# Paired query-key products, one pool of PSUM banks in two-bank tiles, and a new order of work in an adaLN attention and token-MLP block

## Chip, cores and metric

One core of one Trainium2 chip runs the whole block. The time is the device time of one execution in microseconds; a program's time is the median of its runs. Where a sentence below or in the prediction speaks of a span, it is the profiled execution's, from the first to the last thing in the trace.

## What is computed

The input x has 2048 rows of 512. With B = 1, 32 heads of 16, a window of 8 keys at distances 0, 2, ..., 14:

```
sa, ca, ga, sb, cb, gb = silu(c) @ w_mod
h = layernorm(x) * (1 + ca) + sa
q, k, v = h @ wqkv                              # 32 heads of 16
logits[s, w] = q[s] . k[s - 2 w] / 4            # w = 0..7, rows before the first masked
x = x + ga * ((softmax(logits) . v[s - 2 w]) @ wo)
h = layernorm(layernorm(x) * (1 + cb) + sb)
u = gelu(h^T @ w1 + b1)                         # over rows: 2048 -> 1792
x = x + gb * (u @ w2 + b2)^T                    # 1792 -> 2048
```

## The kernel before

Rows are held in 16 tiles of 128 (tile 0 is rows 0 to 127). Attention goes by five chunks of 2, 4, 4, 4 and 2 tiles (`SIZES`), numbered 0 to 4. In each chunk:

- PE (TensorE) makes q, k and v in 512-column products (lines 701 to 742); ACT (ScalarE) and a few times DVE (VectorE) bring them from PSUM to SBUF ("ev" in the names).
- DVE multiplies q with the eight shifted k, once for each of four groups of head dimensions (`qk3_2` is group 2 of chunk 3, line 758 on): 128x4096 elements an instruction in chunks of 4 tiles, 128x2048 in those of 2. PE sums the groups (`red`, 775) into the logits, two banks `psL` that no other work uses.
- DVE takes the maximum (`max`, 794), PE subtracts it (`sub`), ACT takes the exponential (`exp`), PE and ACT make the reciprocal (`esum`, `rcp`), DVE scales (`smB`).
- Four small copies (`a2`, 826) spread the weights, and DVE multiplies them with v (`pv`), PE sums over the window (`pvacc`), ACT brings the result to SBUF (`oev`).
- PE makes the output projection of a tile (`wo`), ACT or DVE adds the gated residual (`x1`); with the residual left out of the projection (suffix n), DVE adds it.
- Then come the second norm: statistics (`ln2q`), root (`rstd2`), bias (`nb2`), the norm (`n2`), the scale and shift of DVE (`aff`, 903, one entry of two instructions); and the third norm (`ln3s`, `rstd3`, `nb3`, `h3`).

MLP1 (922 to 984) sums over rows. Its 14 column tiles f of 128 go in two sweeps of seven, each over parts of the rows; a sum that is interrupted is parked: ACT or DVE copies it from PSUM to SBUF (`park`), and it is put back by PE (`inj`) or added by DVE (`padd`). ACT applies gelu at the end. MLP2 (986 to 1042) makes 16 output tiles, DVE finishes each (`fin`, two instructions), and SP (SyncE) issues the store (`st_out`).

Two tables set the order. `ORDER` (192 to 250) is a list of tokens, written out, of all operations: `:a`, `:d`, `:p`, `:s` name the engine, `:q` has PE do a product as four of 32 columns side by side (lines 541 to 545), n leaves the residual out, `fill:n` is n dummy products. The program is emitted in that order, engine by engine. `schedule()` (86 to 126) gives each operation that needs a PSUM bank the slot that was freed longest ago (line 116). The pool of slots has six banks, each a tile of its own (`psS0` to `psS5`, line 313):

```
psS = [psp.tile([P, 512], F32, name=f"psS{i}") for i in range(6)]
psL = psp.tile([P, 2, 512], F32, name="psL")
```

The framework then makes the semaphore waits between engines from the tiles that instructions read and write.

Of the kernel before, what the change touches and what calls it, by code (L numbers as in the profile page):

```python
# [211 lines left out]
pvacc1_2 qkv3_10:q halo_v3:a oev1_2:a ev3_10:a qkv3_02:q qkv3_20:q pv1_1 qkv3_01:q pvacc1_1 esum2:q ev3_02:a ev3_20:a
ev3_22:a aff0 pv1_0 qkv3_03:q qkv3_00:q pvacc1_0 pv1_3 oev1_1:a ev3_01:a rcp2 halo_k3:a smB2 ln3s0 qkv3_11:q oev1_0:a
pvacc1_3 ev3_11:a oev1_3:a qkv3_23:q fill:1:q wo5:q wo3:q qk3_2 qk3_1 ld_w1_0_0 ld_w1_0_512 vd2_3 xt14 vd2_2 vd2_1
a2_2_1:s a2_2_0:s a2_2_2:s vd2_0 a2_2_3:s wo4:q ln3s1 ev3_03:a ev3_00:a qk3_0 x1_3:a x1_4:a qk3_3 ln2q3 ln2q4 x1_5:a
ev3_23:a qkv4_22:q qkv3_21:q ev3_21:a wo2:q red3_0 x1_2:a qkv4_20:q fill:2:q red3_1 qkv4_00:q red3_2 ev4_22:a ln2q5
ln2q2 ev4_20:a rstd2_2 pv2_0 rstd2_4 red3_3 pvacc2_0 oev2_0:a pv2_3 qkv4_12:q ev4_12:a qkv4_02:q nb2_2 ev4_02:a n2_2:a
max3 sub3:q pvacc2_3 exp3 esum3:q oev2_3:a rstd3_0 pv2_2 nb2_4 pvacc2_2 qkv4_10:q rcp3 n2_5:a oev2_2:a n2_4:a pv2_1
pvacc2_1 fill:4:q oev2_1:a wo6:q wo7:q wo8:q wo9:q ev4_00:a smB3 n2_3:p vd3_3 ld_w1_0_896 vd3_1 vd3_0 a2_3_2:s a2_3_3:s
a2_3_0:s a2_3_1:s vd3_2 ld_w2_1 aff2 nb3_0 aff4 h3_1:p h3_0:p halo_v4:p ln3s3:a ln3s2:d ln3s4:d ln3v3 ln3v2 ln3v4  # L220
ln3s5:a ln3v5 pv3_1 x1_8:a x1_7:a x1_6:a rstd3_2 ev4_10:a h3_3 h3_2 mlp1_0_1_0 mlp1_0_2_0 mlp1_0_5_0:q mlp1_0_3_0:q
pvacc3_1 rstd3_4 nb3_4 x1_9:a pv3_2 pv3_3 pv3_0 h3_4:a h3_5:a oev3_1:a mlp1_0_2_2:q mlp1_0_1_2:q mlp1_0_0_0:q
mlp1_0_0_2:q mlp1_0_3_2:q mlp1_0_0_4:q mlp1_0_5_2:q mlp1_0_5_4:q mlp1_0_3_4:q mlp1_0_1_4:q pvacc3_2 mlp1_0_2_4:q ln2q9
ln2q6 park0_0:a park0_1:a ln2q7 park0_2:a oev3_2:a qk4_0 qk4_2 mlp1_0_4_0:q mlp1_0_4_2:q pvacc3_3 mlp1_0_6_0:q ln2q8
oev3_3:a mlp1_0_6_2:q pvacc3_0 mlp1_0_6_4:q mlp1_0_4_4:q oev3_0:a mlp1_0_7_0:q wo13:qn red4_0 rstd2_6 nb2_6 park0_3:a
qk4_1 x1_13:d n2_9:a n2_6:a park0_4:a wo12:q n2_8:p ld_w1_0_1152 ld_w1_0_1408 vd4_1 ld_w2_3 vd4_2 vd4_0 vd4_3 n2_7:d
qk4_3 wo11:q red4_1 red4_2 red4_3 ln2q13 x1_12:a ln2q12 park0_5:a x1_11:a rstd2_12 aff6 ln3s7:a mlp1_0_9_0 mlp1_0_9_2
mlp1_0_8_0 mlp1_0_9_4 wo10:n max4 nb2_12 sub4 exp4 park0_6:a ln3s9:d ln3s8:d ln3v8 ln3v9 esum4 ln3s6:d ln3v7 rcp4 ln3v6
smB4 rstd3_6 mlp1_0_7_2 mlp1_0_8_2 mlp1_0_10_0 mlp1_0_10_2 mlp1_0_12_0 mlp1_0_12_2 mlp1_0_8_4 mlp1_0_10_4 mlp1_0_7_4
mlp1_0_12_4 a2_4_1:s a2_4_2:s a2_4_3:s n2_13:p x1_10:d nb3_6 h3_8:d h3_6:d h3_7:d a2_4_0:a h3_9:a ln2q10 ln2q11  # L230
rstd2_10 n2_12:d aff12 mlp1_0_11_0 mlp1_0_11_2 mlp1_0_11_4 mlp1_0_8_6 mlp1_0_7_6 pv4_1 nb2_10 pv4_2 pv4_0 ln3s13
# [10 lines left out]
padd2_1 gelu1 gelu4 mlp1_2_3_11 mlp1_2_3_14 mlp1_2_2_14 mlp1_2_6_11 padd2_3 padd2_2 gelu2 padd2_6 gelu6 gelu3
mlp1_1_12_10 mlp1_2_5_11 mlp1_2_5_14 mlp1_1_11_10 padd2_5 padd1_11 gelu5 gelu9 padd1_12 mlp1_1_13_10 gelu12 gelu11
mlp2_0_0 padd1_13 gelu13 ld_w2_4 ld_w2_2 ld_w2_5 mlp2_0_0b ld_w2_7 ld_w2_9 ld_w2_11 ld_w2_13 mlp2_2_0 mlp2_6_0
mlp2_0_0c mlp2_3_0 mlp2_8_0 mlp2_4_0 fin0_0 st_out0_0 fin4_0 fin2_0 st_out2_0 fin6_0 st_out4_0 fpre gsc mlp2_9_0 fin3_0
fin8_0 st_out8_0 st_out6_0 mlp2_5_0 mlp2_1_0 fin1_0 mlp2_14_0 mlp2_10_0 st_out1_0 st_out3_0 fin5_0 ld_w2_15 fin10_0
# [7 lines left out]
def kernel(  # L254
# [379 lines left out]
    def build_chunk(ch):  # L634
# [126 lines left out]
        for dlo in range(4):  # L761
            s_ = _Slot("big")

            def prod(s_=s_):
                return big_r[s_.i][:, 0:NW * C].rearrange("p (q w s) -> p q w s", q=4, w=NW)

            def f(dlo=dlo, prod=prod):
                qv = _ap(q_sb[:, dlo, 0:1], [[0, NW], [SB, 4], [1, SB]])
                kv = _ap(k_c[:, dlo, PAD:PAD + 1], [[-DIL, NW], [SB, 4], [1, SB]])
                nc.vector.tensor_tensor(_ap(prod()[:, 0, 0, 0:1], [[SB, NW], [NW * SB, 4], [1, SB]]), qv, kv,  # L770
                                        op=ALU.mult)
            add("dve", _t_tt2(NW * C), f, reads=[("q", bq, dlo), ("k", ch, dlo), ("kq", ch)] + ([("kh", 3)] if ch == 3 else [("k", ch - 1, dlo)]), alloc=s_,
                locks=True, name=f"qk{ch}_{dlo}")

            def f(dlo=dlo, prod=prod):
                for hf in range(NW // WPM):
                    for jj in range(4):
                        nc.tensor.matmul(psL[32 * jj:32 * jj + 32, hf, 0:WPM * SB], lhsT=group4[:],
                                         rhs=prod()[:, jj, hf * WPM:(hf + 1) * WPM, :], start=(dlo == 0),
                                         stop=(dlo == 3), tile_position=(0, 32 * jj))  # L780
# [297 lines left out]
```

## Time and profile before

| what | value |
|---|---|
| median of 3 runs | 198.61 us (198.4 to 198.69) |
| profiled execution | 198.75 us, span 197.0 us, granted clock 0.997 |
| PE busy | 185.8 us of the span |
| DVE busy | 157.3 us |
| ACT busy | 127.1 us |
| POOL (GpSimd) busy | 22.8 us |
| moved by DMA | 36.02 MB |

All instructions are issued by one helper, so lines of the profile carry the line number 143; groups are told apart by their tiles: big holds DVE's products, psS the PSUM banks, gT the parked sums, h, hT and the like the norms. PE is the matmul engine and PEld its weight loads, which overlap it. A column "idle before" with "<-" names what ended the wait of an engine.

### The profile page before, as it was taken

To read this page: it belongs to the slowest core of one execution; us is meant where nothing else is said; L and a number is where in the kernel's file an instruction comes from. 1 tells how busy PE (TensorE), PEld (TensorE's weight loads), DVE (VectorE), ACT (ScalarE), POOL (GpSimd) and SP (SyncE) were. 2 spreads that over 40 slices of the span, in tenths; PEclk is the share of its full clock that TensorE was granted. 3 is DMA by queue.
4 is the path that set the end of the run, shared out by engine and by line. 5 is a ranking of instruction groups with operands and counts; after the bars stand their busy time and mean duration, and the time that the engine had idled before them with its cause. 6 is when DMAs were issued, how large, how long until landed. Compare 5 with 4: busy or idle time off the path is not lost.

```text
span 197.0 us, 5568 instructions
## 1 busy us (share of the span) xinstructions
PE 185.8 (94%) x2331; PEld 99.5 (50%) x2343; DVE 157.3 (80%) x222; ACT 127.1 (64%) x304; POOL 22.8 (12%) x46
## 2 busy tenths in 40 slices
PE   3999999999999996899999999999999999999993
PEld 1476656565465674435554454444444444444462
DVE  2789999999999999999999999977550207864693
ACT  4799999898999999999997899735660000000000
POOL 4184003000500001130031000500000000000000
PEclk9999999999999999999999999999999999999998
DMA  5999695888997449180497494588999200144113
GB/s 156 357 355 341 226 259 137 101 201 253 302 303 268 149 144 322 34 218 14 136 245 208 91 255 97 157 273 177 290 348 339 61 0 15 38 130 99 53 53 107
DMA packets 53893, 36.02 MB, mean 183 GB/s; under 512 B 24428, under 2 KB 50668, under 8 KB 53868
## 3 DMA queue, kind: packets, MB, share of 16 engines
q1 hardware_dynamic: 52772, 35.27, 64.2%
q10 hardware_dynamic: 1096, 0.39, 0.8%
q8 instruction: 18, 0.29, 0.6%
q14 instruction: 7, 0.06, 0.1%
HBM read 22.55 MB, written 2.10 MB: 125 GB/s over the span
## 4 chain that ended last, share of the span: by engine, by line
PE 63%; DVE 21%; issue 5%; DMA 4%; SPq 3%; ACT 2%; DVEq 0%; ACTq 0%
PE psS L143 61%; DVE big L143 14%; DMA xx<-in_A_x_dram 4%; DVE h L143 4%; SPq L143 3%; PE psL L143 2%; DVE lsb L143 1%; DVE st L143 1%; ACT xx L143 1%; ACT junk L143 1%; DVE m L143 1%; DVE nb L143 0%; ACT k_f L143 0%; DVE woq L143 0%; ACT rs L143 0%
## 5 line engine op out<-in xcount | busy, mean ns | idle before, releaser
L143 PEld LDWEIGHTS <-wst 128*128 128x128 bf16 (+1 forms) x578 | 35.6, 101 | 32.7 <-issue 2.8
L143 PE MATMUL psS<-h,wst 128*32 128x512 bf16 (+1 forms) x350 | 50.1, 379 | 0.4 <-issue 0.2
L143 DVE TENSOR_TENSOR big<-a2sb,vD 128x4096 bf16<-128x4096 bf16 (+1 forms) x20 | 36.4, 1857 | 0.1
L143 DVE TENSOR_TENSOR big<-q_sb,k_f 128x4096 bf16<-128x4096 bf16 (+1 forms) x20 | 36.3, 1857 | 0.0
L143 PE MATMUL psS<-hT,w_qkv 128*32 128x512 bf16 (+1 forms) x576 | 29.0, 344 | 0.0
L143 DVE SCALAR_TENSOR_TENSOR h<-psS,bcol,rows_bc 128x512 f32<-128x512 f32 (+2 forms) x17 | 12.1, 709 | 21.2 <-PE psS L143 21.0
L143 PEld LDWEIGHTS <-w_qkv 128*32 128x32 bf16 (+1 forms) x618 | 21.2, 107 | 13.9
L143 PE MATMUL psS<-gT,big 128*128 128x512 bf16 x111 | 24.8, 379 | 0.1
L143 POOL TENSOR_SCALAR h<-xx,rs,nb 128x512 bf16<-128x512 bf16 x11 | 11.5, 1047 | 94.3 <-DVE nb L143 40.6
L143 PEld LDWEIGHTS <-big 128*128 128x128 bf16 x144 | 12.1, 98 | 13.8 <-DMA big<-in_w_mod_dram 0.5
L143 PE MATMUL psS<-woq,o_sb 128*32 128x512 bf16 (+1 forms) x220 | 16.7, 379 | 0.3 <-ACT o_sb L143 0.3
L143 ACT ACTIVATE gT<-psS,bcol 128x512 bf16<-128x512 f32 x14 | 8.9, 685 | 8.6 <-DVE psS L143 8.6
L143 DVE TENSOR_TENSOR psS<-psS,gT 128x512 f32<-128x512 f32 x14 | 9.4, 697 | 5.5 <-PE psS L143 5.5
L143 DVE TENSOR_TENSOR h<-h,xx 128x512 bf16<-128x512 f32 (+2 forms) x17 | 11.1, 652 | 2.6 <-DMA out_dram<-h 2.1
L143 PE MATMUL psS<-hT,wst 128*32 128x512 bf16 (+2 forms) x134 | 11.8, 355 | 0.2
L143 DVE TENSOR_TENSOR h<-h,rows_bc 128x1024 bf16<-128x1024 bf16 (+2 forms) x16 | 11.5, 718 | 0.5
L143 ACT ACTIVATE v_sb<-psS,qvb 128x512 bf16<-128x512 f32 (+1 forms) x20 | 11.1, 599 | 0.7 <-PE psS L143 0.7
L143 DVE BATCH_NORM_STATS2 st<-xx 128x6 f32<-128x512 bf16 x12 | 7.9, 681 | 4.5 <-DMA xx<-in_A_x_dram 4.5
L143 PEld LDWEIGHTS <-group 128*32 128x32 bf16 x288 | 7.7, 96 | 7.3 <-DVE big L143 1.7
L143 PE MATMUL psS<-big,group 128*32 128x512 bf16 (+1 forms) x160 | 9.9, 338 | 1.1 <-DVE big L143 0.8
L143 ACT ACTIVATE q_sb<-psS,qvb 128x512 bf16<-128x512 f32 (+1 forms) x18 | 10.6, 614 | 0.4 <-PE psS L143 0.3
L143 PEld LDWEIGHTS <-o_sb 128*32 128x32 bf16 (+1 forms) x220 | 7.0, 97 | 7.1 <-ACT o_sb L143 0.8
(106 smaller groups left out, 249.3 us busy)
## 6 DMA issues: line engine op xcount, KB each, us to landing
vD<-v_sb SPq DMA_DIRECT2D x12, 524.5 KB, 5.1
big<-in_B_w_dram SPq DMA_DIRECT2D x4, 896.0 KB, 8.3
vD<-v_sb SPq DMA_DIRECT2D x8, 268.5 KB, 2.5
wst<-in_B_w_dram SPq DMA_DIRECT2D x3, 640.0 KB, 4.4
out_dram<-h SPq DMA_DIRECT2D x15, 128.0 KB, 1.8
wst<-in_B_w_dram SPq DMA_DIRECT2D x2, 800.0 KB, 5.4
xx<-in_A_x_dram SPq DMA_DIRECT2D x6, 256.0 KB, 7.2
gT<-in_w_mod_dram SPq DMA_DIRECT2D x4, 384.0 KB, 7.6
```

The source lines that it names most:

```text
L143: r = fn(*a, **k)
```

## The change

Four things change.

1. *Pairs.* In chunks 3 and 4 one DVE instruction makes the products of two groups (128x8192 and 128x4096 elements); the product lies in the order window, row in all chunks, so the reduction reads it in runs of 128. The ring of four product buffers becomes two tiles of two.
2. *Scale and shift singly.* `aff` becomes `afm` and `afs`, so that other DVE work can stand between them.
3. *One pool of PSUM banks.* The pool has eight slots in four tiles of two banks, psT0 to psT3: slot i is half i mod 2 of tile i div 2. Logits take one slot in chunks 0 and 4, and an aligned pair in the others, instead of `psL`.
4. *Order.* Tokens up to the first output projection (`wo1`) are as before; behind it the list is new. `wo11` and `wo12` leave the residual to DVE, two more of chunk 3's copies and one other of chunk 4's go out from ACT, more products are done four-way.

```
-    G = _Graph(dict(ps=6, big=NBIG, vd=NVD))
+    G = _Graph(dict(ps=8, big=NBIG, vd=NVD))
...
-    psS = [psp.tile([P, 512], F32, name=f"psS{i}") for i in range(6)]
-    psL = psp.tile([P, 2, 512], F32, name="psL")
+    psT = [psp.tile([P, 2, 512], F32, name=f"psT{i}") for i in range(4)]
 
     def ps(slot):
-        return psS[slot.i][:]
+        return psT[slot.i // 2][:, slot.i % 2, :]
...
-    big_r = ring(NBIG, [P, NW * CM], BF, "big")
+    big_t = ring(NBIG // 2, [P, 2, NW * CM], BF, "big")
+    big_r = [big_t[i // 2][:, i % 2, :] for i in range(NBIG)]
...
+        NQ = 2 if ch in QKP else 1
+        for d0 in range(0, 4, NQ):
+            s_ = _Slot("big", NQ * C // CM or 1)
...
+            def f(d0=d0, prod=prod):
+                qv = _ap(q_sb[:, d0, 0:1], [[C, NQ], [0, NW], [1, C]])
+                k0, k1 = k_c[:, 0, PAD:PAD + 1], k_c[:, 1, PAD:PAD + 1]
+                kv = _ap(k_c[:, d0, PAD:PAD + 1], [[k1.offset - k0.offset, NQ], [-DIL, NW], [1, C]])
+                nc.vector.tensor_tensor(prod(), qv, kv, op=ALU.mult)
...
-                nc.vector.tensor_tensor(hv, hv, ab_bc[:].unsqueeze(1).to_broadcast([P, gn, D]), op=ALU.mult)
-                nc.vector.tensor_tensor(hv, hv, sb_bc[:].unsqueeze(1).to_broadcast([P, gn, D]), op=ALU.add)
...
+            for nm, row, rk, op_ in (("afm", ab_bc, "ab_bc", ALU.mult), ("afs", sb_bc, "sb_bc", ALU.add)):
...
-x1_1:a wo0:q x1_0:a ln2q1 xt10 xt12 red2_0 qkv2_23:q qkv3_22:q qkv3_12:q vd1_0 st_row1 vd1_2 ev2_23:a ln2q0 rstd2_0
...
+st_row1 vd1_1 vd1_2 xt10 ld_row1 a2_1_3:s a2_1_0:s xt12 a2_1_2:s vd1_3 vd1_0 red2_0 wo1:q x1_1:a wo0:q ln2q1 qkv2_21:q
...
```

The rows below are the program's, in each engine's order; the numbers behind names tell buffers apart, and "waits" names the engine whose work a row waits for.

*PE, before the first qkv product* (ident alone is a filler, ident and h a transpose of the normed rows, hT and wst the product). In the kernel before:

```order
L143 MATMUL psS2_65<-ident_108,h3_76 128x128
L143 LDWEIGHTS ident_108
L143 MATMUL psS3_66<-ident_108 128x512
...
L143 MATMUL psS3_66<-ident_108,h3_76 128x128
...
L143 LDWEIGHTS wst2_107 [waits DMAHW7_49]
L143 MATMUL psS5_68<-hT0_77,wst2_107 128x256 [waits Activation_49]
```

And in the changed kernel, at the same place:

```order
L146 MATMUL psT1_64<-ident_103,h3_73 128x128
L146 LDWEIGHTS ident_103
L146 MATMUL psT1_64<-ident_103 128x512 [waits Activation_49]
...
L146 MATMUL psT1_64<-ident_103,h3_73 128x128 [waits Activation_49]
...
L146 LDWEIGHTS wst2_102 [waits DMAHW7_49]
L146 MATMUL psT2_65<-hT0_74,wst2_102 128x256 [waits Activation_49]
```

The order is the same; the filler and the second tile's transposes lie in the other half of the tile that ACT reads, and wait for ACT.

*DVE, from the second tile's hT to the first query-key product* (hT from PSUM, statistics of x, q from PSUM, then big<-q_sb,k_f). Before:

```order
L143 TENSOR_SCALAR hT1_78<-psS4_67,a1col_111 128x512 [waits Activation_49]
L143 SCALAR_TENSOR_TENSOR nb_0_130<-mv_0_127,rs_0_129 128x4 [waits DVE_49,Activation_49]
L143 TENSOR_SCALAR hT1_78<-psS3_66,a1col_111 128x512
L143 BN_STATS st6_0_126<-xx_70 128x6 [waits DMAHW3_49]
L143 BN_STATS st6_0_126<-xx_70 128x6
L143 BN_STATS st6_0_126<-xx_70 128x6 [waits DMAHW4_49]
L143 BN_AGGR mv_0_127<-st6_0_126 128x2 [waits DVE_49] x2
L143 TENSOR_TENSOR q_sb0_79<-psS5_68,qvb_119 128x512 [waits Activation_49]
```

After:

```order
L146 TENSOR_SCALAR hT1_75<-psT2_65,a1col_106 128x512 [waits PE_49,Activation_49]
L146 SCALAR_TENSOR_TENSOR nb_0_125<-mv_0_122,rs_0_124 128x4 [waits DVE_49,Activation_49]
L146 TENSOR_SCALAR hT1_75<-psT1_64,a1col_106 128x512 [waits PE_49]
L146 BN_STATS st6_0_121<-xx_67 128x6 [waits DMAHW3_49]
L146 BN_STATS st6_0_121<-xx_67 128x6
L146 BN_STATS st6_0_121<-xx_67 128x6 [waits DMAHW4_49]
L146 BN_AGGR mv_0_122<-st6_0_121 128x2 [waits DVE_49] x2
L146 TENSOR_TENSOR q_sb0_76<-psT2_65,qvb_114 128x512 [waits PE_49,Activation_49]
```

Nothing moved; two of the reads now wait for PE's work on the other half, the second of them for the bias product of q and v (`qvb0`), with the statistics queued behind it.

*ACT, around the second norm of chunk 2* (xx<-psS is x1, junk<-xx a statistic, lv and rs the root, v_sb, k_f and q_sb evictions, h2 the norm). Before:

```order
L143 ACTIVATE xx_70,sums_125<-psS1_64 128x512 [waits PE_49,Pool_49]
L143 ACTIVATE junk_123,sums_125<-xx_70,sums_125 128x512 [waits Activation_49]
L143 ACTIVATE v_sb0_82<-psS0_63,qvb_119 128x512 [waits DMAHW3_49,DMAHW1_49,PE_49]
L143 ACTIVATE junk_123,sums_125<-xx_70,sums_125 128x512 [waits Activation_49]
L143 ACTIVATE lv_1_133<-sums_125,epscol_110 128x2 [waits Activation_49]
L143 ACTIVATE rs_1_134<-lv_1_133 128x2 [waits Activation_49]
L143 ACTIVATE v_sb0_82<-psS3_66,qvb_119 128x512 [waits PE_49]
L143 ACTIVATE h3_76<-xx_70,nb_0_130,rs_0_129 128x512 [waits DVE_49]
L143 ACTIVATE k_f_81<-psS4_67 128x512 [waits PE_49]
L143 ACTIVATE h20_103<-xx_70,nb_1_135,rs_1_134 128x512 [waits DVE_49]
```

After:

```order
L146 ACTIVATE xx_67,sums_120<-psT0_63 128x512 [waits Pool_49]
L146 ACTIVATE junk_118,sums_120<-xx_67,sums_120 128x512 [waits Activation_49]
L146 ACTIVATE v_sb0_79<-v_sb1_80 128x4x16
L146 ACTIVATE lv_1_128<-sums_120,epscol_105 128x2 [waits Activation_49]
L146 ACTIVATE rs_1_129<-lv_1_128 128x2 [waits Activation_49]
L146 ACTIVATE k_f_78<-k_f_78 128x4x16 [waits DVE_49]
L146 ACTIVATE v_sb0_79<-psT1_64,qvb_114 128x512 [waits PE_49]
L146 ACTIVATE v_sb0_79<-psT0_63,qvb_114 128x512
L146 ACTIVATE h20_98<-xx_67,nb_1_130,rs_1_129 128x512 [waits DVE_49]
```

The two copies of borders (16 columns) moved to ACT ahead of the norm, and a v eviction whose tile's other half holds `qkv3_11` (`ev2_20`) stands ahead of it too.

*ACT and PE at the start of MLP1's second sweep* (gT is a park; junk<-h a statistic of the third norm). ACT in the changed kernel:

```order
L146 ACTIVATE gT_71<-psT3_66 128x512
L146 ACTIVATE lv_1_128<-mv_1_127,epscol_105 128x1 [waits DVE_49]
L146 ACTIVATE rs_1_129<-lv_1_128 128x1 [waits Activation_49]
L146 ACTIVATE junk_118,mv_2_132<-h20_98 128x512 [waits DVE_49]
L146 ACTIVATE junk_118,st6_2_131<-h20_98 128x512 [waits Activation_49]
L146 ACTIVATE lv_2_133<-mv_2_132,epscol_105 128x1 [waits DVE_49]
L146 ACTIVATE rs_2_134<-lv_2_133 128x1 [waits Activation_49]
L146 ACTIVATE gT_71<-psT2_65 128x512 [waits PE_49]
```

Before, the parks stand ahead of that statistic:

```order
L143 ACTIVATE o_sb_102<-psS5_68 128x512 [waits PE_49]
L143 ACTIVATE gT_74<-psS0_63 128x512
L143 ACTIVATE o_sb_102<-psS3_66 128x512 [waits PE_49]
L143 ACTIVATE gT_74<-psS4_67 128x512
L143 ACTIVATE junk_123,mv_2_137<-h21_104 128x512 [waits DVE_49,Activation_49]
```

The park of f 12 (the last row of the first piece) moved behind the norm of tile 14, and PE's product of f 3 in the second sweep lies in the other half of its tile, psT2.

More of the change, by code (lines that the diff above doesn't have):

```diff
@@ L115, in schedule @@
                 p = o.alloc.pool
-                o.alloc.i = min((freed[p][k], k) for k in range(self.pools[p]) if held[p][k] is None)[1]
-                held[p][o.alloc.i] = o.alloc
+                z = o.alloc.size
+                o.alloc.i = min((max(freed[p][k:k + z]), k) for k in range(0, self.pools[p] - z + 1, z)
+                                if held[p][k:k + z] == [None] * z)[1]
+                held[p][o.alloc.i:o.alloc.i + z] = [o.alloc] * z
             if o.frees is not None:
@@ L120, in schedule @@
                 if o.frees.left == 0:
-                    held[o.frees.pool][o.frees.i] = None
-                    freed[o.frees.pool][o.frees.i] = pos
+                    z, k = o.frees.size, o.frees.i
+                    held[o.frees.pool][k:k + z] = [None] * z
+                    freed[o.frees.pool][k:k + z] = [pos] * z
             done.add(o.idx)
@@ L212 @@
[L212 to L231, printed above, removed]
@@ L242 @@
[L242 to L246, printed above, removed]
@@ new lines @@
+ev2_21:a x1_0:a ln2q0 qkv2_22:q halo_v2:a qkv2_20 fill:2:q red2_1 qkv2_23:q red2_2 red2_3 qkv3_02:q qkv3_11:q rstd2_0
+halo_k3:a ev2_20:a nb1_4 nb2_0 ev2_22:a n2_0:a n2_1:a pv1_2 max2 qkv3_21:q sub2:q n1_15:a ev2_23:a exp2 pvacc1_2
+oev1_2:a ev3_11:a n1_14:p afm0 pv1_0 afs0 pv1_1 qkv3_00 ev3_02:a ev3_00:a qkv3_03:q esum2:q qkv3_01:q pvacc1_0
+qkv3_10:q qkv3_12 pvacc1_1 ln3s0 ev3_01:a rcp2 ev3_10:a pv1_3 qkv3_13:q fill:3:q ev3_21:a oev1_1:a oev1_0:a halo_v3:a
+pvacc1_3 oev1_3:a smB2 vd2_1 vd2_0 vd2_3 xt14 a2_2_2:s a2_2_3:s a2_2_1:s vd2_2 a2_2_0:s qk3_0 ev3_13:a ev3_03:a
@@ new lines @@
+fin2_0 fin0_0 ld_w2_7 ld_w2_9 ld_w2_11 ld_w2_15 st_out0_0 st_out2_0 ld_w2_13 mlp2_1_0:q mlp2_10_0 mlp2_6_0 fin1_0
+fin3_0 st_out3_0 st_out1_0 mlp2_4_0 mlp2_9_0 fin4_0 mlp2_8_0 mlp2_13_0 mlp2_7_0 fin6_0 st_out6_0 fin5_0 st_out5_0
+fin9_0 fin10_0 st_out4_0 fin8_0 st_out8_0 st_out9_0 mlp2_14_0 mlp2_11_0 fin7_0 fin13_0 st_out10_0 st_out7_0 fpre
+fin11_0 st_out11_0 st_out13_0 fin14_0 mlp2_12_0 fin12_0 st_out14_0 st_out12_0 mlp2_15_0 fin15_0 st_out15_0 mlp2_15_1
+fin15_1 st_out15_1 mlp2_15_2 fin15_2 st_out15_2
@@ L284 @@
     INJ=(1,),
+    QKP=(3, 4, ),
+    PVP=(),
     CENT=((0, 14), (2, 0), (2, 12)),
@@ L548, in fill_fn @@
         for r in [4] * (n // 4) + [1] * (n % 4):
-            mm(psS[k][:, 0:r * P], lhsT=ident[:], rhs=ident[:].unsqueeze(1).to_broadcast([P, r, P]), start=True, stop=True)
+            mm(psT[k // 2][:, k % 2, 0:r * P], lhsT=ident[:], rhs=ident[:].unsqueeze(1).to_broadcast([P, r, P]), start=True, stop=True)
     G.fill_fn = fill_fn
@@ L759, in build_chunk @@
                 desc=9, alloc=s_)
-        for dlo in range(4):
-            s_ = _Slot("big")
-            def prod(s_=s_):
[L765 to L780, printed above, removed]
-            add("pe", 0.02 + NW // WPM * _t_mm(WPM * SB), f, reads=["consts", "big_use"], frees=s_, writes=["psL"],
-                name=f"red{ch}_{dlo}", tiled=True)
@@ new lines, in build_chunk, with lps, f @@
+        s_L = _Slot("ps", NW // WPM)
+        def lps(hf, s_L=s_L):
+            return psT[(s_L.i + hf) // 2][:, (s_L.i + hf) % 2, :]
+        NQ = 2 if ch in QKP else 1
+        for d0 in range(0, 4, NQ):
+            s_ = _Slot("big", NQ * C // CM or 1)
+            def prod(s_=s_):
+                return _ap(big_t[s_.i // 2][:, s_.i % 2, 0:1], [[NW * C, NQ], [C, NW], [1, C]])
+            def f(d0=d0, prod=prod):
[3 more added lines that the diff above has]
+                nc.vector.tensor_tensor(prod(), qv, kv, op=ALU.mult)
+            add("dve", _t_tt2(NQ * NW * C), f, reads=[x for d_ in range(d0, d0 + NQ) for x in [
+                ("q", bq, d_), ("k", ch, d_)] + ([] if ch == 3 else [("k", ch - 1, d_)])] + [("kq", ch)] + (
+                    [("kh", 3)] if ch == 3 else []), alloc=s_, locks=True, name=f"qk{ch}_{d0}")
+            for dlo in range(d0, d0 + NQ):
+                def f(dlo=dlo, d0=d0, s_=s_):
+                    pr = _ap(big_t[s_.i // 2][:, s_.i % 2, 0:1], [[C, NW], [1, C]]) if dlo == d0 else _ap(
+                        big_t[s_.i // 2][:, s_.i % 2, NW * C:NW * C + 1] if NQ * C < 2 * CM else big_t[s_.i // 2][:, 1, 0:1],
+                        [[C, NW], [1, C]])
+                    for hf in range(NW // WPM):
+                        for jj in range(4):
+                            nc.tensor.matmul(lps(hf)[32 * jj:32 * jj + 32, 0:WPM * SB], lhsT=group4[:],
+                                             rhs=pr[:, hf * WPM:(hf + 1) * WPM, jj * SB:(jj + 1) * SB], start=(dlo == 0),
+                                             stop=(dlo == 3), tile_position=(0, 32 * jj))
+                add("pe", 0.02 + NW // WPM * _t_mm(WPM * SB), f, reads=["consts", "big_use"], frees=s_,
+                    name=f"red{ch}_{dlo}", tiled=True,
+                **(dict(alloc=s_L) if dlo == 0 else dict(writes=[s_L])))
```

72 lines of the change are left out of this document (44 added, 28 removed).

## The prediction

> **What bounds the kernel now.** I read the page's shares first, then busy time by stage, then the chain of waits.
>
> ```profile
> span 197.0 us, 5568 instructions
> PE 185.8 (94%) x2331; PEld 99.5 (50%) x2343; DVE 157.3 (80%) x222; ACT 127.1 (64%) x304; POOL 22.8 (12%) x46
> PE 63%; DVE 21%; issue 5%; DMA 4%; SPq 3%; ACT 2%; DVEq 0%; ACTq 0%
> ```
>
> PE's 94% is an average over stages with different limits. The table by stage (us; PE, PEld, DVE, ACT, POOL busy; clock; DMA) separates them:
>
> ```profile
> 16.00:40.00 24.00, 23.86 (x544) 14.56 (x548) 23.50 (x25) 22.74 (x53) 2.52 (x4) 1.00 0.78 208
> 40.00:64.00 24.00, 23.79 (x480) 13.52 (x476) 23.96 (x18) 22.88 (x53) 2.94 (x2) 1.00 0.98 269
> 64.00:76.00 12.00, 11.01 (x288) 7.81 (x280) 12.00 (x7) 11.76 (x34) 0.77 (x1) 1.00 0.60 183
> 76.00:88.60 12.60, 10.37 (x199) 4.97 (x200) 12.40 (x18) 12.04 (x33) 2.44 (x3) 1.00 0.56 164
> 88.60:145.00 56.40, 55.97 (x480) 27.08 (x486) 49.78 (x88) 44.17 (x105) 5.53 (x6) 1.00 0.71 183
> 145.00:191.00 46.00, 45.79 (x213) 21.12 (x216) 22.39 (x33) 1.84 (x3) 0.00 (x0) 1.00 0.36 105
> ```
>
> From 16 to 88.6 us DVE has no gap: attention's products run end to end, and PE and ACT, nearly as full, fill in around them. From 88.6 to 191 PE has no gap and DVE has. So a delay of DVE before 88.6, or of PE behind it, goes whole into the time. There is no slack in which three nearly full engines could absorb new waits on one another.
>
> **The new waits.** The diff speaks of one pool of banks. The order rows show what that costs: four tiles of two banks stand where six tiles of one stood, and the program's semaphore waits now go by tile. Of 222 waits between instructions on one of the four tiles, 120 are between its two halves, where no data pass. None of these exists in the kernel before, whose six banks are tiles of their own. They begin with the program's first transposes, where the order of work is otherwise unchanged. A bound for one: nothing if the other half's work is long done, otherwise the rest of that work. An eviction or a park is the nearest row:
>
> ```profile
> L143 ACT ACTIVATE k_f<-psS 128x512 bf16<-128x512 f32 x16 | 9.4, 589 | 0.5 <-PE psS L143 0.3 <-issue 0.2
> L143 ACT ACTIVATE v_sb<-psS,qvb 128x512 bf16<-128x512 f32 x12 | 7.9, 683 | 0.7 <-PE psS L143 0.7
> L143 ACT ACTIVATE gT<-psS 128x512 bf16<-128x512 f32 x14 | 8.0, 587 | 0.2 <-PE psS L143 0.2
> L143 DVE TENSOR_TENSOR psS<-psS,gT 128x512 f32<-128x512 f32 x14 | 9.4, 697 | 5.5 <-PE psS L143 5.5
> ```
>
> So 120 waits cost between nothing and about 120 x 0.6 = 72 us; and where the other half's work stands behind something else in its queue, that comes on top. I walked the changed order by hand, with the durations of these rows.
>
> **Start, to the first product: +6.6 us.**
>
> ```profile
> 9.09 1.24 PE L143 MATMUL psS<-ident 128*128 128x512 bf16 x5
> 10.47 2.71 ACT L143 ACTIVATE hT<-psS,a1col 128x256 bf16<-128x256 bf16 x6
> 11.71 2.93 PE L143 MATMUL psS<-hT,wst 128*128 128x256 bf16 x24
> 13.87 0.48 DVE L143 TENSOR_SCALAR hT<-psS,a1col 128x512 bf16<-128x512 bf16 x1
> 14.47 0.54 PE L143 MATMUL psS<-sc,big 128*128 128x1 bf16 x16
> 14.60 1.88 DVE L143 BATCH_NORM_STATS2 st<-xx 128x6 f32<-128x512 bf16 x3 [0.26 <-DMA xx<-in_A_x_dram]
> 14.88 1.05 PE L143 MATMUL psS<-hT,wst 128*128 128x256 bf16 x8
> 15.76 0.67 PE L143 MATMUL psS<-sab,wst 128*128 128x1 bf16 x16
> 16.67 0.69 DVE L143 TENSOR_TENSOR q_sb<-psS,qvb 128x512 bf16<-128x512 f32 x1
> 17.46 1.23 DVE L143 TENSOR_TENSOR big<-q_sb,k_f 128x2048 bf16<-128x2048 bf16 x1
> ```
>
> Before, five fillers run at 9.09 while PE waits for h, and the first qkv product at 11.71. Now the fillers (half 1 of psT1) wait for ACT's first reads of half 0, which begin at 10.47: about 11.7 to 13.0. The next read of hT waits for them (to 13.5), the second tile's transposes for that read (to 14.4), ACT's read of those takes until 15.3, and the qkv product, in the other half of psT2, stands behind it: 15.35, or 3.65 late. Its 2.93 and the modulation's 0.54 end at 18.8; the q product now waits for ACT to read sab: 18.95 to 20.0; the bias product takes 0.67, to 20.7. Only then may DVE read hT, which it did at 13.87. Queued behind that on DVE are three statistics (1.88), an aggregate and q's eviction (0.69): 20.7 + 0.48 + 1.88 + 0.23 + 0.69, with 0.07 of handoff, gives 24.05 for the first product, against 17.46.
>
> **To the last product of chunk 2: +8.85.** The order of DVE is the old one up to here.
>
> ```profile
> 24.48 0.69 DVE L143 TENSOR_REDUCE m<-psL 128x64 bf16<-128x512 f32 x1
> 33.26 1.22 DVE L143 TENSOR_REDUCE m<-psL 128x128 bf16<-128x1024 f32 x1 [0.28 <-PE psL L143]
> 42.44 0.68 DVE L143 TENSOR_TENSOR lsb<-lsb,rb 128x1024 bf16<-128x1024 bf16 x1
> 61.05 0.68 DVE L143 TENSOR_TENSOR lsb<-lsb,rb 128x1024 bf16<-128x1024 bf16 x1
> 80.54 0.68 DVE L143 TENSOR_TENSOR lsb<-lsb,rb 128x1024 bf16<-128x1024 bf16 x1
> 86.22 2.29 DVE L143 TENSOR_TENSOR big<-a2sb,vD 128x4096 bf16<-128x4096 bf16 x1
> ```
>
> The first maximum comes at 32.5 (from 24.48, +8.0, since its tile's other half holds a product and an eviction of k or q), the second at 41.5 (from 33.26), the softmax scaling of chunk 1 at 51.3 (from 42.44).
>
> **To the last value products of chunk 3: +23.4.** PE reaches the first output projection at 56.9, because three evictions ahead of it hang on the other half. ACT's row for x1_0 comes late, hence rstd2_0, and nb2_0 stops DVE for 3.2 us. Then ACT stands at ev2_20 until PE's qkv3_11 is through; the two norms of chunk 2 are queued behind it, and DVE's scale (afm0) waits 3.2 for them. With 1.75 in smaller waits chunk 2's scaling comes at 78.05 (from 61.05, +17.0). The scaling of chunk 3 then waits 3.65 for ACT's reciprocal, and 2.75 come in smaller ones: the value product of 86.22 starts at 109.6.
>
> The edit named first gains little against that. Two products per instruction save one start each:
>
> ```profile
> L143 DVE TENSOR_TENSOR big<-q_sb,k_f 128x4096 bf16<-128x4096 bf16 x12 | 26.9, 2282 | 0.0
> L143 DVE TENSOR_TENSOR big<-q_sb,k_f 128x2048 bf16<-128x2048 bf16 x8 | 9.4, 1219 | 0.0
> ```
>
> 2 x 1.219 - 2.282 = 0.156 us is the most that a start is worth (ends overlap the next start), so 4 instructions save up to 0.6; the first and last reductions wait for a pair, 1.1 to 2.3 us later, under the other products. Scale and shift were two instructions before, and stay two: 0, or a slot for another instruction between them. I take -0.3 for both; the range is -0.6 to +2.3.
>
> Two more of chunk 3's copies of the weights go out from ACT's queue, and reductions read their product in runs of 128:
>
> ```profile
> L143 SPq DMA_DIRECT2D a2sb<-lsb x17: 609/642/1692, 29.9 to 109.7; - x17
> L143 ACTq DMA_DIRECT2D a2sb<-lsb x3: 617/629/745, 29.9 to 108.4; - x3
> L143 PE MATMUL psL<-big,group 128*32 128x512 bf16 x128 | 9.3, 379 | 0.0
> L143 PE MATMUL psL<-m,nident 128*32 128x512 bf16 x28 | 2.2, 381 | 1.3 <-DVE m L143 1.3
> ```
>
> On ACT that is 2 x 0.63 = 1.3 us ahead of its statistics, and on SP as much less, so the last copy could land 1.3 sooner or ACT be 1.3 later. DVE's scale, shift and statistics fill 81.1 to 86.2 before and hide either; I take 0, and 1.3 each way for the range. A read in runs of 128 is in the trace (nident: 381 against 379 ns): 0.002 on each of 160 matmuls, 0.
>
> **MLP1: +19 on PE.** PE has no gap here before, so each wait counts. Those that I find, in order: the tile of f 4 for the reductions beside it 2.8; f 7 for a park 1.45; the subtraction of chunk 4 0.6; f 10 0.95; f 9 0.95; a value reduction of chunk 4 for two parks 1.25; an output projection 0.85; f 3 of the second sweep 4.85; f 8 of it 1.45; then four in the last sweep and the reduction ahead of it, 0.95, 1.1, 1.75 and 0.6 (estimates in steps of one eviction, or one and its PE product). Together 19.6, say 19. The 4.85 is the case to remember: PE needs half 1 of psT2, ACT's park of half 0 stands behind a statistic and a root of chunk 4's last norm, and these behind DVE.
>
> **MLP2: +1.3.** One wait of 1.75 for a finished output in the other half. The new order ends with two stores fewer in the last rush:
>
> ```profile
> 193.65 0.29 DVE L143 TENSOR_TENSOR h<-psS,fpre 128x128 bf16<-128x128 f32 x1
> 192.07 2.75 SPq L143 DMA_DIRECT2D out_dram<-h  x6
> ```
>
> SP issues six stores from 192.07 to 194.82, 0.46 each, while DVE is done at 193.94: at most one store, 0.45, can be gained. PE's own work shrinks by 2.25 matmuls of 512 columns; at 45.79 / 213 = 0.215 us that is -0.5. It is eaten by more changes between whole and four-way matmuls:
>
> ```profile
> 85.88 0.39 PE L143 MATMUL psS<-xx,ident 128*32 128x512 bf16 x4
> 86.20 2.17 PE L143 MATMUL psS<-h,wst 128*128 128x512 bf16 x19
> ```
>
> Such a change takes 0.32 to the next start, 0.10 over the 0.215; there are 14 more, 4 of them where PE is the bound: +0.4, and 1.4 if DVE's cover over the other ten is gone.
>
> **The sum.** 23.4 to the value products, 19 on PE, 1.75, less 0.45, and -0.1 for work and changes: +43.6 on the span of 197.0, rounded down to 43 because my waits gate a few instructions whole of which only a part is held. The profiled execution took 198.75, and the median of the runs shown is 198.61, 0.1% less: **242 us**. Handoffs of 0.2 us that turn out to be 0.3 on about 100 waits would add 10; if half the stalls on PE are refilled, 10 go: 230 to 254 for this case by itself.
>
> **The rivals.** *Partly hidden.* The first start is late by 6.6 (its chain has no other work to hide in), but behind it the waits are mostly met in time, since both halves are used in turn; half of MLP1's 19 remain: 198.75 + 6.6 + 9.5 = 215; from 207 to 228 by what 16 to 88 us adds. Against it stand the three full engines of the table. *Faster.* More banks in one pool let PE run ahead: PE's gaps between 64 and 88.6 are 0.99 + 2.23 = 3.2 us; half of it refilled, 0.45 at the stores and 0.5 of work less give 196.3. It decides at the first transposes: PE must start its first qkv product by 11.7, which needs the fillers not to wait for ACT. The order rows say that they do. *Not what it says.* The waits are there but always met, the pairs save nothing that DVE's successor can use: 198.75 - 0.5 + 0.4, or 198.6.
>
> The Trainium skill, "PSUM — Partial Sum Buffer", in "Terms", bars two engines only from one bank and quadrant at a time; two halves of a tile are two banks. By that rule none of the 120 waits is needed, and the time would be the last rival's 198.6 or the faster one's 196.3. The rule speaks of what the banks bear, not of which waits a program holds; no trace here shows yet what they cost. The skill's "Perfetto Trace Analysis", in "Matmul Optimizations", wants all eight banks in use; that is the faster rival's mechanism.
>
> **How the numbers follow.** Forecast 0.70; partly hidden 0.20; faster 0.05; not what it says 0.05. A range from 214 to 256 leaves out the last two and half a tenth on either side: 8 in 10. A measurement here can tell 0.2% (0.4 us) from no change: faster 0.06, within 0.03, slower 0.91.
>
> **What would show it.** In the profile after: the first 128x2048 product near 24 us, not 17.5; gaps on DVE in 16 to 110 us that ACT and PE end, of 15 us together; PE's share near 78%, with gaps of 0.6 to 5 us whose releasers are ACT evictions and DVE adds of other tiles' halves; MLP2 from about 187. A first product at 17.5 would sink the forecast at its first step; gaps on DVE without gaps on PE behind 110 would make it the partly hidden case.

## The result and the profile after

The changed kernel takes 247.77 us (median of 4 runs, 244.5 to 250.1) against 198.65 for the kernel before: a ratio of 1.2415, 95% interval 1.2367 to 1.2464. One of the four runs, that of 250.1, counts as slow, and the ratio is of the other three. The kernel is slower by 49 us; the forecast was 242. The profiled execution is the 244.5 one, at a granted clock of 0.986.

Its page, first the span and busy times, then the chain of work that ended last:

```profile
span 242.7 us, 5619 instructions
PE 193.4 (80%) x2348; PEld 101.7 (42%) x2361; DVE 160.0 (66%) x223; ACT 127.1 (52%) x302; POOL 20.2 (8%) x46
PE 37%; ACT 9%; DVE 6%; issue 2%; DMA 1%; SPq 0%; ACTq 0%; DVEq 0%
```

DVE and ACT are about as busy in microseconds as before (160.0 and 127.1 against 157.3 and 127.1), and PE 7.6 us more. So most of the 45.7 us of added span is waiting: 38 of it on PE and 43 on DVE. By stage (PE, PEld, DVE, ACT, POOL; clock):

```profile
0.00:24.00 24.00, 16.27 (x172) 10.29 (x174) 12.84 (x38) 14.63 (x38) 9.56 (x32) 1.00 0.90 291
48.00:72.00 24.00, 18.43 (x325) 10.02 (x314) 14.52 (x12) 13.09 (x32) 0.77 (x1) 0.93 0.55 125
113.00:150.00 37.00, 29.43 (x363) 14.21 (x358) 28.42 (x40) 24.71 (x59) 3.97 (x5) 1.00 0.36 103
150.00:188.00 38.00, 27.57 (x194) 11.95 (x200) 20.75 (x46) 17.35 (x41) 1.54 (x2) 0.96 0.66 173
188.00:236.00 48.00, 46.76 (x243) 21.14 (x241) 23.34 (x34) 2.55 (x4) 0.00 (x0) 1.00 0.30 87
```

Where DVE had no gap before (16 to 88.6) it is now busy 14.5 of 24 us between 48 and 72; where PE had none, it is busy 27.6 of 38 between 150 and 188. Only MLP2, from 190 us on, runs as it did.

The start, on PE (what stands in brackets is the idle time before the row, and what ended it):

```profile
11.59 1.24 PE L146 MATMUL psT<-ident 128*128 128x512 bf16 x5 [1.29 <-ACT hT L146]
13.39 1.05 PE L146 MATMUL psT<-ident,h 128*128 128x128 bf16 x16 [0.56 <-ACT hT L146]
15.22 2.78 PE L146 MATMUL psT<-hT,wst 128*128 128x256 bf16 x24 [0.78 <-ACT hT L146]
18.75 1.03 PE L146 MATMUL psT<-hT,wst 128*128 128x256 bf16 x8 [0.37 <-ACT sab L146]
```

And on DVE:

```profile
20.33 0.48 DVE L146 TENSOR_SCALAR hT<-psT,a1col 128x512 bf16<-128x512 bf16 x1 [3.41 <-PE psT L146]
22.66 0.66 DVE L146 TENSOR_TENSOR q_sb<-psT,qvb 128x512 bf16<-128x512 f32 x1
23.43 2.36 DVE L146 TENSOR_TENSOR big<-q_sb,k_f 128x2048 bf16<-128x2048 bf16 x2
```

A filler that reads only a constant waits for ACT's read of hT: that is a wait between halves, seen. The chain of the forecast is there link by link, with the first product at 23.43 (24.05 was forecast, 17.46 it was). Further on DVE:

```profile
63.75 0.16 DVE L146 SCALAR_TENSOR_TENSOR nb<-sums,rs 128x2 f32<-128x2 f32 x1 [2.68 <-ACT rs L146]
71.27 0.69 DVE L146 TENSOR_TENSOR h<-h,rows_bc 128x1024 bf16<-128x1024 bf16 x1 [3.20 <-ACT h L146]
79.08 0.68 DVE L146 TENSOR_TENSOR lsb<-lsb,rb 128x1024 bf16<-128x1024 bf16 x1
104.12 0.69 DVE L146 TENSOR_TENSOR lsb<-lsb,rb 128x1024 bf16<-128x1024 bf16 x1 [3.15 <-ACT rb L146]
109.81 2.29 DVE L146 TENSOR_TENSOR big<-a2sb,vD 128x4096 bf16<-128x4096 bf16 x1
```

On PE, from MLP1 on, the longest gaps and MLP2's first product, and that product in the kernel before:

```profile
115.00 1.05 PE L146 MATMUL psT<-h,wst 128*32 128x512 bf16 x16 [1.62 <-ACT xx L146]
125.86 0.61 PE L146 MATMUL psT<-h,wst 128*32 128x512 bf16 x8 [1.82 <-ACT gT L146]
159.39 1.90 PE L146 MATMUL psT<-h,wst 128*32 128x512 bf16 x16 [4.81 <-ACT gT L146]
169.40 5.12 PE L146 MATMUL psT<-h,wst 128*128 128x512 bf16 x23 [1.41 <-DVE gT L146]
185.01 5.02 PE L146 MATMUL psT<-h,wst 128*128 128x512 bf16 x58 [1.87 <-ACT gT L146]
189.97 0.39 PE L146 MATMUL psT<-gT,w_qkv 128*128 128x512 bf16 x1
```

```profile
145.04 0.38 PE L143 MATMUL psS<-gT,w_qkv 128*128 128x512 bf16 x1
```

The releasers are ACT's parks and gelu (gT) and DVE's additions. Whether such a wait is one for data or one between halves the profile alone doesn't say; the experiments do.

### The profile page after: what moved, and what is told of

It reads as the page before. It is cut to its first block, busy times and chain, and to the rows that moved or that the text cites. A ratio compares the mean times of both kernels' runs of the same rounds, so it can differ in the third digit from the quotient of the medians.

```text
span 242.7 us, 5619 instructions
## 1 busy us (share of the span) xinstructions
PE 193.4 (80%) x2348; PEld 101.7 (42%) x2361; DVE 160.0 (66%) x223; ACT 127.1 (52%) x302; POOL 20.2 (8%) x46
## 4 chain that ended last, share of the span: by engine, by line
PE 37%; ACT 9%; DVE 6%; issue 2%; DMA 1%; SPq 0%; ACTq 0%; DVEq 0%
PE psT L146 37%; ACT gT L146 3%; ACT junk L146 2%; DVE h L146 2%; DVE psT L146 2%; ACT xx L146 1%; DMA out_dram<-h 1%; ACT o_sb L146 1%; ACT lv L146 1%; ACT h L146 1%; ACT rs L146 1%; DVE big L146 0%; DVE xx L146 0%; ACT v_sb L146 0%; DVE gT L146 0%
## 5 line engine op out<-in xcount | busy, mean ns | idle before, releaser
L146 PE MATMUL psT<-h,wst 128*32 128x512 bf16 (+1 forms) x460 | 53.4, 389 | 16.3 <-ACT gT L146 10.0
L146 PEld LDWEIGHTS <-wst 128*32 128x32 bf16 (+1 forms) x686 | 36.3, 101 | 52.6 <-issue 24.0
L146 PE MATMUL psT<-hT,w_qkv 128*32 128x512 bf16 (+3 forms) x516 | 32.4, 361 | 11.8 <-ACT q_sb L146 4.2
L146 DVE TENSOR_TENSOR big<-q_sb,k_f 128x4096 bf16<-128x4096 bf16 (+2 forms) x16 | 36.0, 2287 | 2.8 <-ACT q_sb L146 2.0
L146 DVE SCALAR_TENSOR_TENSOR h<-psT,bcol,rows_bc 128x512 f32<-128x512 f32 (+2 forms) x17 | 12.1, 710 | 21.7 <-PE psT L146 21.4
L146 PE MATMUL psT<-gT,big 128*128 128x512 bf16 x110 | 25.0, 379 | 1.1 <-DVE h L146 1.0
L146 PE MATMUL psT<-big,group 128*32 128x512 bf16 (+1 forms) x288 | 18.9, 358 | 3.1 <-ACT k_f L146 1.9
L146 PE MATMUL psT<-woq,o_sb 128*32 128x512 bf16 (+1 forms) x194 | 16.3, 380 | 4.1 <-ACT o_sb L146 3.6
L146 ACT ACTIVATE v_sb<-psT,qvb 128x512 bf16<-128x512 f32 (+1 forms) x20 | 11.3, 598 | 7.7 <-PE psT L146 7.1
L146 PE MATMUL psT<-hT,wst 128*32 128x512 bf16 (+2 forms) x134 | 11.8, 356 | 1.9 <-ACT hT L146 0.8
```

The costliest lines, as they stand in the source:

```text
L146: r = fn(*a, **k)
```

## The experiments

The first theory is the forecast's: the waits between the two halves of a tile cost the time. The rivals are that the new order, or the pairs, cost it.

**Banks apart.** Six of the eight slots become tiles of one bank; the pair that takes logits stays one tile, and single users take its slots last.

```
-    psT = [psp.tile([P, 2, 512], F32, name=f"psT{i}") for i in range(4)]
+    psL = psp.tile([P, 2, 512], F32, name="psL")
+    psS = [psp.tile([P, 512], F32, name=f"psS{i}") for i in range(6)]
+
+    def bank(i):
+        return psL[:, i, :] if i < 2 else psS[i - 2][:]
```

> The changed kernel with its order, its pairs and its eight slots, but six slots are tiles of one bank and only the two that take logits share a tile; single users take those two last. If the waits between halves cost the time: 198.6 +- 2 us, first product at 17.5 us, PE at 90% or more. If the new order or the pairs cost it: 215 us or more, with the first product early and gaps further on. If half and half: about 220.

Measured: 204.87 us (the kernel before, beside it: 199.07), ratio 1.0285 (1.0247 to 1.0324). DVE's first product and the value product that was 23.6 late:

```profile
17.32 1.23 DVE L147 TENSOR_TENSOR big<-q_sb,k_f 128x2048 bf16<-128x2048 bf16 x1
86.86 2.29 DVE L147 TENSOR_TENSOR big<-a2sb,vD 128x4096 bf16<-128x4096 bf16 x1
```

The first comes where it came before, the second 0.64 later than before; the order and the pairs are the changed kernel's. So 43 of the 49 us go with the tiles. But 6 us were left, three times what I expected. On PE they are gaps behind 88 us, among them:

```profile
92.81 0.62 PE L147 MATMUL psS<-big,group 128*32 128x512 bf16 x8 [0.93 <-ACT xx L147]
126.70 1.05 PE L147 MATMUL psS<-h,wst 128*32 128x512 bf16 x16 [1.85 <-ACT gT L147]
140.64 2.32 PE L147 MATMUL psS<-h,wst 128*128 128x512 bf16 x10 [1.59 <-DVE gT L147]
```

In MLP1 single users do get the shared tile, which may cost these; or the new order itself does. The longest of the three, 1.85 us, is not a wait between halves. PE's product (f 3 of the second sweep) goes into slot 4 of `schedule()`, the single tile psS2, and in the built program it waits for the park of f 11, which ACT reads from that same tile:

```profile
126.07 0.58 ACT L147 ACTIVATE gT<-psS 128x512 bf16<-128x512 f32 x1
```

The two slots of the shared tile were free then, but single users take them last. In the changed kernel that product gets slot 5.

**Eight tiles.** This tells the two apart: the changed kernel's order and slots, each slot a tile. Logits in two slots are then taken half by half.

```
-    psT = [psp.tile([P, 2, 512], F32, name=f"psT{i}") for i in range(4)]
+    psE = [psp.tile([P, 512], F32, name=f"psE{i}") for i in range(8)]
...
+            for hf in range(NW // WPM):
+                nc.vector.tensor_reduce((m2_t[:, 0:SB] if hf else m1).unsqueeze(1), _ap(lps(hf)[:, 0:1], [[1, SB], [SB, WPM]]),
+                                        mybir.AxisListType.X, ALU.max)
+            if NW // WPM == 2:
+                nc.vector.tensor_tensor(m1, m1, m2_t[:, 0:SB], op=ALU.max)
```

> The changed kernel with the same order and the same slots, each of the eight a tile of its own; the maximum and the exponential of a pair of logits go half by half (three more DVE and one more ACT instruction in each of three chunks, some 0.4 us of DVE a chunk). No wait between banks is left. If the 6 us that the kernel with banks apart still lost came from the one tile that two slots share: 200 +- 1 us. If they come from the order or the pairs: 204 to 206.

Measured: 200.13 us, ratio 1.0055 (1.0037 to 1.0073). With the same slots and order, and no shared tile, 48 of the 49 us are gone. The two stages where the changed kernel lost most are full again:

```profile
40.00:64.00 24.00, 23.83 (x452) 12.29 (x443) 23.96 (x19) 22.52 (x52) 2.75 (x1) 1.00 0.91 219
88.60:145.00 56.40, 55.92 (x594) 26.11 (x602) 50.45 (x90) 43.63 (x108) 5.49 (x7) 1.00 0.62 163
```

So the order and the pairs are not what banks apart still lost: five of its six us go with its one shared tile, through waits between the halves or, as in the gap of 1.85, through the rule that spares this tile. No run separates these two. The last 1.1 us include the split itself: two reductions of 686 ns for one of 1218, with one combination each, in three chunks. The product buffers are joined in twos here as in the changed kernel, so what waits that adds lies within these 1.1 us too.

**The kernel before, paired.** The reverse: one thing added to the kernel before.

```
-    psS = [psp.tile([P, 512], F32, name=f"psS{i}") for i in range(6)]
+    psT = [psp.tile([P, 2, 512], F32, name=f"psT{i}") for i in range(3)]
+    psS = [psT[i // 2][:, i % 2, :] for i in range(6)]
```

> The kernel before with one thing changed: its six single banks are the halves of three tiles. If the waits between halves cost the time: 20 to 50 us slower, first product near 24 us. If only the new order makes such waits bind: within 2 us of the kernel before.

Measured: 254.9 us, ratio 1.2818 (1.2753 to 1.2883), with the first product late like the changed kernel's:

```profile
23.83 2.36 DVE L143 TENSOR_TENSOR big<-q_sb,k_f 128x2048 bf16<-128x2048 bf16 x2
```

Three lines of tile declaration, with neither pairs nor new order, cost 56 us, somewhat more than I had allowed. Together with eight tiles this settles the cause from both sides.

**Far halves.** Is it that the slot freed longest ago puts neighbours in time into one tile? Here slots i and i + 4 share one, and a pair of logits takes such two.

```
-        return psT[slot.i // 2][:, slot.i % 2, :]
+        return psT[slot.i % 4][:, slot.i // 4, :]
```

> The changed kernel with the same order and four tiles of two banks, but slots i and i + 4 share a tile, not slots 2 i and 2 i + 1; so neighbours in time lie in different tiles. If what a wait costs is that the slot freed longest ago puts consecutive work into one tile: half or less of the loss, 205 to 225 us. If any sharing of a tile costs as much: 240 to 255.

Measured: 250.84 us, ratio 1.2587 (1.2553 to 1.2621). The expectation of half the loss fell. The first product does come sooner, but it brings nothing at the end:

```profile
20.73 2.36 DVE L152 TENSOR_TENSOR big<-q_sb,k_f 128x2048 bf16<-128x2048 bf16 x2
```

Why a neighbour four places off costs as much as the next one is not shown. It is not that all slots are held at once: along the list, a slot is handed out with four of the eight held on average, and with all eight in 4 of 153 cases.

**Late start.** Does a late first product go whole into the time? In the kernel before it is done six times, with the same values.

```
+                for _ in range(6 if (ch, dlo) == (0, 2) else 1):
```

> The kernel before, whose first query-key product on DVE is done six times over (the same values): some 5.6 us more at the head of DVE's chain, where the changed kernel was 6.0 late. If a late start goes whole into the time: 204 +- 1 us. If gaps behind it take it up: under 201.

Measured: 205.77 us, ratio 1.0341 (1.0311 to 1.037), 6.7 us (6.2 to 7.4 by the interval). DVE's products of chunk 0, in the kernel before and here:

```profile
17.46 4.63 DVE L143 TENSOR_TENSOR big<-q_sb,k_f 128x2048 bf16<-128x2048 bf16 x4
```

```profile
17.66 10.93 DVE L143 TENSOR_TENSOR big<-q_sb,k_f 128x2048 bf16<-128x2048 bf16 x9
```

The repeats cost 6.3 us, not the 5.6 that I had reckoned, and all of it arrives. The table by stage shows PE's clock at half in the stretch behind the gap that this leaves on PE:

```profile
26.00:28.00 2.00, 1.64 (x28) 1.24 (x31) 2.00 (x3) 0.00 (x0) 0.00 (x0) 0.50 0.00 0
28.00:30.00 2.00, 2.00 (x32) 1.11 (x24) 2.00 (x3) 1.19 (x5) 0.00 (x0) 0.50 0.03 8
```

**Late start, gap filled.** The same with dummy matmuls in PE's gap.

```
-ev1_00:a ln1s14 ev1_13:a qkv1_03:q red0_0 qkv0_22:q ln1v12 rstd1_3 ev1_03:a qvb_cp1:a qkv1_11:q red0_1 red0_2 red0_3
+ev1_00:a ln1s14 ev1_13:a qkv1_03:q fill:80 red0_0 qkv0_22:q ln1v12 rstd1_3 ev1_03:a qvb_cp1:a qkv1_11:q red0_1 red0_2 red0_3
```

> The kernel with the late start (the first product done six times), with 20 dummy matmuls of 512 columns (4.3 us) on PE in the gap of 4.5 us that the late start leaves there. If the half clock that PE had for some 6 us behind that gap comes from the gap and cost time: the clock stays near 1.00 there and the time falls by 1 to 1.5 us, to about 204.5. If the half clock has another cause or its work lies under DVE: the same time as without them, 205.8.

Measured: 205.45 us, ratio 1.0327 (1.0297 to 1.0357). The clock is whole in the same stretch:

```profile
24.00:26.00 2.00, 2.00 (x11) 0.92 (x10) 1.97 (x3) 0.00 (x0) 0.00 (x0) 1.00 0.02 9
28.00:30.00 2.00, 1.98 (x45) 1.07 (x38) 2.00 (x3) 0.88 (x3) 0.00 (x0) 1.00 0.28 57
```

So the half clock does come from the gap. The time stays the same within the intervals, as it would if PE's slower work lies under DVE's here.

**Parks first.** Does PE's gap of 4.81 count whole? In the changed kernel, the parks of f 11 and f 12 go ahead of the last norms on ACT.

```
-... afs14 park0_11:a rstd2_15 ... rstd3_14 park0_12:a afs15
+... park0_10:a park0_11:a park0_12:a ln3s12 ...
```

> The changed kernel with two parks (f 11 and f 12) ahead of the norms of the last tiles on ACT. If PE's gap of 4.8 us near 155 us is that park's wait and PE's time goes whole into the end: the gap is gone and MLP2 starts 3 to 4.8 us earlier. If the next wait takes its place: under 1 us. (The run to run spread of the changed kernel is 2%, so the profile decides.)

Measured: 250.65 us (248.21 to 254.68), ratio 1.2537 (1.2453 to 1.2621), not faster than the changed kernel's 1.2415. The profiled execution ran at a clock of 0.919, so only its gaps are read here:

```profile
157.93 2.96 PE L146 MATMUL psT<-h,wst 128*32 128x512 bf16 x48
161.05 6.01 PE L146 MATMUL psT<-h,wst 128*128 128x512 bf16 x26 [0.16 <-issue]
168.47 5.33 PE L146 MATMUL psT<-h,wst 128*128 128x512 bf16 x23 [1.41 <-DVE gT L146]
176.00 6.19 PE L146 MATMUL psT<-h,wst 128*128 128x512 bf16 x20 [2.20 <-DVE gT L146]
184.87 2.63 PE L146 MATMUL psT<-h,wst 128*128 128x512 bf16 x11 [2.68 <-ACT gT L146]
190.96 5.24 PE L146 MATMUL psT<-h,wst 128*128 128x512 bf16 x34 [3.46 <-ACT gT L146]
```

The gap of 4.81 is gone, and those behind it are longer: 2.20, 2.68 and 3.46 where the changed kernel has 1.00, 0.60 and 1.87. From chunk 3's last value products to MLP2, PE's gaps are 19.1 us together here and 18.8 in the changed kernel. The times say that nothing was gained by taking away one wait out of many. That the waiting moved is read from one profile at a lower clock, which may have a part in it.

**Pairs undone, banks apart.** The first experiment's kernel with the products one by one.

```
-    QKP=(3, 4, ),
+    QKP=(),
```

> The same with the pairs undone (each pair as two instructions, one behind the other). If a start of a DVE instruction is all that pairs save: 0.2 to 0.6 us slower than the kernel with banks apart and pairs. If pairs make the reductions late: faster by up to 2 us.

Measured: 205.61 us (204.78 to 206.6), ratio 1.0316 (1.0275 to 1.0357), against 204.87 (204.45 to 205.63). The difference of 0.7 has the sign of the forecast's 0.2 to 0.6 and is a little above it, but the intervals overlap, and the two profiled spans are 203.8 and 203.9. A pair of 128x4096 takes 4.41 us where two single ones take 2 x 2.28, but ends overlap: three single ones in a row take 6.68 us and two pairs 8.75, so their starts are 2.20 and 4.34 apart, and a pair saves some 0.06.

```profile
L147 DVE TENSOR_TENSOR big<-q_sb,k_f 128x8192 bf16<-128x8192 bf16 x2 | 8.7, 4411 | 0.0
```

**Stores first.** The kernel before with the stores of tiles 12 and 14 ahead of that of 13.

```
-mlp2_13_0 fin13_0 st_out13_0 st_out12_0 st_out14_0 mlp2_15_0
+mlp2_13_0 st_out12_0 st_out14_0 fin13_0 st_out13_0  mlp2_15_0
```

> The kernel before with two stores (tiles 12 and 14) put ahead of the last additions on SP. If SP's queue sets the end by 0.45 us, as the prediction has it: 0.4 us faster. If the last store waits for DVE or for its landing: the same.

Measured: 198.66 us against 199.05 for the kernel before, ratio 0.9982 (0.9962 to 1.0001). SP's last two stores are issued from 193.55 to 194.36, where the kernel before had its last three from 193.46 to 194.82:

```profile
193.55 0.81 SPq L143 DMA_DIRECT2D out_dram<-h  x2
```

The span is 196.6 against 197.0. The 0.4 us are about the forecast's 0.45, but the interval just reaches 1, so this is likely and not shown. It is the only kernel here that may beat the kernel before.

## Why the prediction was right

The direction, the cause and most of the sizes held. Term by term, in the profiled executions:

| term | forecast | measured | from |
|---|---|---|---|
| first product | +6.6 | +5.97 | 23.43 against 17.46 |
| scaling of chunk 2 | +17.0 | +18.0 | 79.08 against 61.05 |
| DVE's wait for rstd2_0 | 3.2 | 2.68 | row at 63.75 |
| DVE's wait for the norms | 3.2 | 3.20 | row at 71.27 |
| DVE's wait for the reciprocal | 3.65 | 3.15 | row at 104.12 |
| value product of chunk 3 | +23.4 | +23.59 | 109.81 against 86.22 |
| PE's wait for the park of f 12 | 4.85 | 4.81 | row at 159.39 |
| MLP1 in all | +19 | +21.3 | 189.97 against 145.04, less 23.59 |
| MLP2 | +1.3 | +1.15 | DVE's last row, 239.73 against 193.65, less 44.93 |
| span | +43.6 | +45.7 | 242.7 against 197.0 |

It was right for the reason given: the built program's waits were read, not the diff's description. Eight tiles (1.0055) and the kernel before in paired tiles (1.2818) show that these waits are the cause. The banks themselves did not need them: the Trainium skill, "PSUM — Partial Sum Buffer", bars two engines only from one bank and quadrant at a time in "Terms", and the trace of eight tiles agrees, with PE busy for 187.8 and ACT for 125.4 of its 198.0 us. The time of the neutral rival came within 1.1 us for this kernel, whose tiles are single banks.

Three things were off. *MLP1's term* was 2.3 us too small, though not in its waits: PE's gaps from 109.8 to 190 us are 18.8 together, where 19.6 was walked and the kernel before has 0.45. The rest is PE's own work taking longer, some 1.5 us of it by the half clock behind the gap of 4.81. The reasoning was weaker than the size: the forecast counted each wait whole, since PE had no gap before. Parks first speaks against this for single waits: with 4.81 taken away, no time was gained. Walked in order, as the forecast did, the sum comes out; as a price list of waits to be removed, it does not. *The clock* was missing. PE is busy 193.4 us where the same order in eight tiles takes 187.8, and the clock, which falls behind some gaps (last section), has a part in that. At 0.986, 1.4% of 242.7 us or 3.4 us is clock that was not granted; at 0.972, in the run of 247.71 us with a span of 246.0, it is 2.8% or 6.9 us. These two runs differ by 3.5 us of clock and 3.3 us of span, so the clock can account for that difference, and the median may lie above the profiled execution for that reason; this is worked out, not tried. *The rest of the change* had been put at about -0.1 in the sum and 198.6 in the neutral rival; with eight tiles it is +1.1 us (0.7 to 1.5), of which the split of the logits is a part. That the new order saves PE's 0.5 us or the stores' 0.45 can't be seen under that.

Two slips in the working move nothing: the -0.3 taken for pairs and single scales is not in the sum, and the faster rival's terms (198.75 less 1.6, 0.45 and 0.5) give 196.2, not 196.3. A start of a DVE instruction, put at 0.156 us at most, came to some 0.06.

The start's carry was right: the late start alone costs the kernel before all of its 6.3 us.

## What to carry to other kernels

Before joining buffers into one tile, look at the waits that the built program makes: where they go by tile, two banks that no data connect become one, and with three engines nearly full, an eviction then often stops the neighbour's producer. To undo it, undo it everywhere: with one shared tile left the kernel still lost some 5 us, a different choice of neighbours cost as much, and taking away the longest single wait gained nothing. And where an engine is full from its first instruction on, expect a late head of its queue to arrive whole at the end, as the 6.3 us did here.
